# A mixture-of-experts stack: the rows of gate factors of four token chunks, built on TensorE or read back from DRAM

## The chip, the cores and the metric

The kernel runs on one core of a Trainium2 chip. The metric is the time of one execution in device microseconds (us), as the median of several executions. TensorE is called PE in the rows below, its weight loads PEld, VectorE DVE, ScalarE ACT, GpSimd POOL, and SyncE, from whose queue nearly all transfers are issued, SP.

## What is computed

Three stages follow each other: a linear attention with positive random features, a mixture of 8 experts of which each token uses one, and a mixture of 4 experts of which each token uses all. Cut to what matters:

```python
# attention: q, k, v are 2 x 8 x 576 x 64; x becomes 1152 tokens x 512
q_p, k_p = phi(q), phi(k)                       # exp(proj - sq - max) / sqrt(128)
x = (q_p @ (k_p^T @ v)) / (q_p . sum(k_p) + 1e-6)
# first mixture: one expert per token
logits = x @ w_gate;  e_idx = argmax(logits, axis=1)
gate_w = softmax(logits)[e_idx];  eom = sigmoid(x @ w_output_gate)
for e in range(8):
    mask = e_idx == e
    out[mask] = gate_w[mask] * eom[mask, e] * (relu(x[mask] @ w1[e]) @ w2[e])
# second mixture: all four experts
out2 = sum_e p[:, e] * (relu(out @ dw1[e]) @ dw2[e])
```

The change touches the factor `gate_w * eom` of the first mixture alone.

## The kernel before

**Tiling.** The 1152 tokens are two sequences (b = 0, 1) of 576, and each is two chunks of 288, so there are four chunks c = 0..3, with b = c // 2. A chunk is 256 main tokens (two groups of 128) and 32 of the rest. Activations lie turned: features on the 128 partitions, tokens along the row. For the first mixture each sequence has a main expert, the one that most of its tokens chose. The kernel runs the whole chunk through its main expert: `unit1` is the first layer (8 blocks f of 128 hidden features, 12 matmuls of 288 columns each), `unit2` or `unit2_blocks` the second (4 blocks d of 128 output features, 24 matmuls each, tiles `py`). Every product is made as three fp32r matmuls of high and low parts, `mm3`. The result of block d is multiplied by the row of gate factors `gb`, which holds at each token the factor of the main expert, or zero where the token chose another. The same 288 numbers stand on all 128 partitions. Tokens of other experts are added afterwards, by a block for one expert with few tokens (`X`, `second`, `scatter`) and by a loop of a run-time count, which no execution here enters (`tc.If(nx > 0)`, L1186).

**How the row of factors is made.** The gate works with tokens on partitions: `sel_factors` (L586) multiplies the gate values by the main expert's one-hot and sums to `sel`, one column for each group of 128 main tokens and one for the rest. `in_parts` (L580) splits it into a high and a low part. `gate_row` (L910) turns it into a row: ACT scales the rows of an identity by the column, which gives diagonals `dg` (six ACTIVATEs a chunk), PE multiplies them by a matrix of ones (two matmuls, L919, tile `pg`), and ACT copies `pg` to `gb` (L921).

**What sets the order.** A tile framework with a scheduler puts each engine's instructions in a row of its own and adds the semaphore waits; parts of the first stage are chained by hand (`pin`). An engine takes its row in order, and so does SP with its DMAs. Before chunk 0's second layer PE does the last blocks of its first layer, the gate logits of sequence 1, and then mixes matmuls of blocks d = 0 and d = 1 with small matmuls `cps`: one that counts tokens by expert (`cps<-gm_eq`, L503, from DVE's `gm_eq`, L496), and one that needs the one-hot `oh_all`, which DVE's gate chain gives (L573, L575). DVE in that stretch does the low parts `wlo` of the second layer's weights, the gate chain of sequence 1, and chunk 0's products with `gb` (L940). After the branch at L1186, SP loads the second expert's weights (`E1.load2`, L143) for chunk 2.

Of the kernel before, what the change touches and what calls it, by code (L numbers as in the profile page):

```python
# [38 lines left out]
def moe_stack(ctx, tc, q, k, v, omega, w_gate, w_ogate, mw1, mw2, dprobs, dw1, dw2, out):  # L39
# [178 lines left out]
    def load_v(b, hh):  # L218
        raw["v", b, hh] = load_main(v, b, hh, "v", G, D + 1)

    xs = ctx.enter_context(tc.tile_pool(name="dp", bufs=1, space=bass.MemoryType.DRAM)).tile([9, 128, DM], F32, name="xs")
    om2 = cp.tile([128, 2, D], F32, name="om2")
    for r in range(2):
        nc.scalar.dma_start(om2[:, r, :], omega)
# [294 lines left out]
    def gate_math(b, lg, mx, eq, m, cb):  # L519
# [44 lines left out]
        if b == 0:  # L564
            sels = [sel_factors(c, b, eng, pn) for c in range(2)]
            yield
            for c in range(2):
                sel0.append(sels[c]())
        yield

    def gate_count(b, psp, tag):
# [2 lines left out]
                         start=True, stop=True)  # L574
        nc.tensor.matmul(ps[:, :, 2], ones_r, ohr[:, 2 * b:2 * b + 2], start=True, stop=True)  # L575
        nc.vector.tensor_reduce(cnt[:, 2 * b:2 * b + 2], ps.rearrange("p c t e -> p c e t"), axis=AX.X, op=ALU.add)

    sel0 = []

    def in_parts(s, p=lambda i: i):  # L580

        p(nc.vector.tensor_copy(s[:, 0].bitcast(F32R), s[:, 1]))
        p(TT(s[:, 1], s[:, 1], s[:, 0], op=ALU.subtract))
        return s

    def sel_factors(c, b, eng, p=lambda i: i):  # L586
        t = cp.tile([128, 3, NE], F32, tag="selt", name="selt", bufs=2)
        bc = ohb[:, b:b + 1, :]
        p(eng.tensor_tensor(t[:, 0:2], g_all[:, 2 * c:2 * c + 2], bc.to_broadcast([128, 2, NE]), op=ALU.mult))
        p(eng.tensor_tensor(t[:, 2:3], grm[:, c:c + 1], bc, op=ALU.mult))  # L590

        def total():
            s = cp.tile([128, 2, 3], F32, tag="sel", name="sel", bufs=2)
            p(nc.vector.tensor_reduce(s[:, 1], t, axis=AX.X, op=ALU.add))
            return in_parts(s, p)
        return total

    def sel_static(c, b):
        return sel_factors(c, b, nc.vector)() if b else sel0[c]


    units = []
# [326 lines left out]
        return l1(w1, xhc, xlc, *(rings or RINGS))  # L929

    def unit2_blocks(c, w2, hs, late=None):
        gb = gate_row(sel_static(c, c // 2))
        for d in range(KB):
            if d == KB - 1 and late is not None:
                late += [l2_block(w2, hs, d, (ps_k, "kv")), gb]
                yield
                return
            y = l2_block(w2, hs, d, (ps_k, "kv") if (c, d) == (0, 0) else None)
            for dst, src in zip(x2cols(c), (slice(0, 256), slice(256, NC))):
                TT(x2T[:, d, dst], y[:, src], gb[:, src], op=ALU.mult)  # L940
            yield

    def unit2(c, w2, hs):
        if c >= 2:
            gb = gate_row(sel_static(c, c // 2))
            return add_out(w2, hs, gb, list(zip(x2cols(c), (slice(0, 256), slice(256, NC)))))
        for _ in unit2_blocks(c, w2, hs):
            pass

    def x2cols(c):  # L950
        return slice(256 * c, 256 * c + 256), slice(1024 + 32 * c, 1056 + 32 * c)
# [8 lines left out]
    def add_out(w2, hs, gb, cols):  # L960
        for d in range(KB):
            add_yt(l2_block(w2, hs, d), gb, d, cols)
# [84 lines left out]
    for _ in blocks:  # L1047
        pass
    nx_t, mt, le_t, lc_t, sel1, wi_t = extras()
    hs = unit1(1, E0.w1)  # L1050
    pool_x = ExitStack()
    xg_ = pool_x.enter_context(tc.tile_pool(name="xg", bufs=1))
# [133 lines left out]
    with tc.If(nx > 0, preferred_fallthrough_block=True, label="more"):  # L1186
        with tc.For_i(0, nx, 1) as it:
# [18 lines left out]
            add_out(xe.w2, hs, gate_row(in_parts(sx)), [(bass.ds(lc * 256, 256), slice(0, 256)),  # L1206
                                              (bass.ds(lc * 32 + 1024, 32), slice(256, NC))])
    add_yt(*last, KB - 1, list(zip(x2cols(1), (slice(0, 256), slice(256, NC)))))
    pool_l.close()
    pool_o.close()  # L1210
    xq = ctx.enter_context(tc.tile_pool(name="xq", bufs=1, side="right"))
# [2 lines left out]
    E1.load2()  # L1214
    hs = unit1(2, E1.w1)
    unit2(2, E1.w2, hs)
    hs = unit1(3, E1.w1)


# [117 lines left out]
    xc.append(pair_of(xr0, [128, KB, GROUPS[0][1]], ("xch", "xcl")))  # L1337
    x_side(0, nc.vector)()
    w2_ahead = [load_w2(0, 0)]
    gb = gate_row(sel_static(3, 1))  # L1340
    for k in range(2):
        for d in (k, k + 2):
            add_yt(l2_block(E1.w2, hs, d), gb, d, list(zip(x2cols(3), (slice(0, 256), slice(256, NC)))))
# [140 lines left out]
```

## Time and profile before

| | us |
|---|---|
| median of 3 executions | 573.23 (573.07 to 573.31) |
| the profiled execution | 572.74 |
| its span (first to last instruction) | 570.8 |
| around the span | 1.94 |
| PE busy | 562.7 |
| DVE busy | 394.5 |
| ACT busy | 251.1 |
| POOL busy | 263.7 |

The profiled execution is 0.49 us under the median. In the span, attention ends at about 84 us, the first mixture lies from there to about 191 us, and the second mixture takes the rest. PE's busy time counts matmuls that overlap; the start of its weight loads (PEld) tells better at what pace it goes, and a stretch in which they follow each other at an even pace is one in which PE waits for nothing.

### The profile page before, as it was taken

To read this page: it belongs to the slowest core of one execution; us is meant where nothing else is said; L and a number is where in the kernel's file an instruction comes from. 1 tells how busy PE (TensorE), PEld (TensorE's weight loads), DVE (VectorE), ACT (ScalarE), POOL (GpSimd) and SP (SyncE) were. 2 spreads that over 40 slices of the span, in tenths; PEclk is the share of its full clock that TensorE was granted. 3 is DMA by queue.
4 is the path that set the end of the run, shared out by engine and by line. 5 is a ranking of instruction groups with operands and counts; after the bars stand their busy time and mean duration, and the time that the engine had idled before them with its cause. 6 is when DMAs were issued, how large, how long until landed. Compare 5 with 4: busy or idle time off the path is not lost.

```text
span 570.8 us, 11664 instructions
## 1 busy us (share of the span) xinstructions
PE 562.7 (99%) x4526; PEld 510.4 (89%) x4527; DVE 394.5 (69%) x865; ACT 251.1 (44%) x622; POOL 263.7 (46%) x318
## 2 busy tenths in 40 slices
PE   8999999999999999999999999999999999999997
PEld 7787899987999999989989999889988999889996
DVE  7877978946669886666676666666666666665664
ACT  5988844135624534344343443334434344343230
POOL 5996464000100327673663846638456375563210
PEclk9999999999999999999999999999999999999999
DMA  7851560483600400220220021022022002000004
GB/s 179 227 151 40 176 207 1 164 293 116 224 1 5 144 2 2 75 74 1 75 73 1 2 75 73 2 73 75 1 74 75 0 29 85 36 2 1 0 1 165
DMA packets 42473, 42.83 MB, mean 75 GB/s; under 512 B 14896, under 2 KB 31792, under 8 KB 42416
## 3 DMA queue, kind: packets, MB, share of 16 engines
q1 hardware_dynamic: 42128, 42.00, 23.4%
q8 instruction: 36, 0.59, 0.4%
q14 instruction: 21, 0.17, 0.1%
q10 hardware_dynamic: 288, 0.07, 0.1%
HBM read 37.34 MB, written 4.72 MB: 74 GB/s over the span
## 4 chain that ended last, share of the span: by engine, by line
PE 75%; DVE 0%; issue 0%
PE po L646 12%; PE po L645 12%; PE po L647 11%; PE pp L647 10%; PE pp L646 10%; PE pp L645 10%; PE ph L645 2%; PE py L645 2%; PE py L647 1%; PE ph L646 1%; PE ph L647 1%; PE py L646 1%; PE pg L919 0%; DVE ob L1436 0%
## 5 line engine op out<-in xcount | busy, mean ns | idle before, releaser
L105 POOL TENSOR_TENSOR wlo<-st,whi 128x512 fp32r<-128x512 f32 x96 | 115.4, 1222 | 178.1 <-ACT whi L104 134.7
L104 ACT CAST whi<-st 128x512 fp32r<-128x512 f32 x116 | 65.6, 590 | 114.6 <-PE po L647 49.3
L646 PE MATMUL po<-wlo,hh 128*128 128x512 f32 x290 | 112.8, 389 | 0.0
L645 PE MATMUL po<-whi,hh 128*128 128x512 f32 x290 | 112.7, 389 | 0.0
L647 PE MATMUL po<-whi,hl 128*128 128x512 f32 x290 | 112.4, 388 | 0.0
L885 POOL TENSOR_TENSOR hl<-c,hh 128x320 fp32r<-128x320 f32 (+1 forms) x64 | 52.1, 814 | 84.7 <-ACT hh L884 66.7
L647 PE MATMUL pp<-xh,wlo 128*128 128x320 f32 (+1 forms) x256 | 75.8, 296 | 0.0
L646 PE MATMUL pp<-xl,whi 128*128 128x320 f32 (+1 forms) x256 | 75.7, 296 | 0.0
L645 PE MATMUL pp<-xh,whi 128*128 128x320 f32 (+1 forms) x256 | 75.6, 295 | 0.0
L1419 DVE SCALAR_TENSOR_TENSOR oa<-po,pb,oa 128x512 f32<-128x512 f32 x75 | 55.1, 747 | 29.1 <-PE po L647 29.1
L647 PEld LDWEIGHTS po<-whi,hl 128*128 128x128 f32 x290 | 54.5, 188 | 11.4
L645 PEld LDWEIGHTS po<-whi,hh 128*128 128x128 f32 x290 | 54.5, 188 | 10.4
L646 PEld LDWEIGHTS po<-wlo,hh 128*128 128x128 f32 x290 | 54.5, 188 | 10.1
L1419 DVE SCALAR_TENSOR_TENSOR ob<-po,pb,ob 128x512 f32<-128x512 f32 x59 | 44.2, 749 | 26.8 <-PE po L647 26.8
L1374 DVE TENSOR_TENSOR c<-u,pp 128x320 f32<-128x320 f32 (+1 forms) x96 | 43.3, 453 | 22.4 <-PE pp L647 21.9
L883 ACT ACTIVATE c<-c 128x320 f32<-128x320 f32 (+1 forms) x64 | 28.5, 445 | 50.7 <-DVE c L1374 50.0
L646 PEld LDWEIGHTS pp<-xl,whi 128*128 128x128 f32 x256 | 48.5, 190 | 1.2
L645 PEld LDWEIGHTS pp<-xh,whi 128*128 128x128 f32 x256 | 48.5, 190 | 1.2
L647 PEld LDWEIGHTS pp<-xh,wlo 128*128 128x128 f32 x256 | 48.5, 190 | 0.0
L641 DVE SCALAR_TENSOR_TENSOR hl<-c,hh 128x320 fp32r<-128x320 f32 (+1 forms) x64 | 44.4, 724 | 0.5 <-ACT hh L640 0.2
L351 ACT ACTIVATE e<-pj,nb 128x128 f32<-128x128 f32 x144 | 39.1, 392 | 6.6 <-DVE nb L342 6.4
L645 PE MATMUL ph<-xh,whi 128*128 128x288 f32 x128 | 38.2, 299 | 0.4 <-PEq L1186 0.4
(280 smaller groups left out, 1248.9 us busy)
## 6 DMA issues: line engine op xcount, KB each, us to landing
st<-in_moe_w_dram SPq DMA_DIRECT2D x36, 512.0 KB, 4.5
st<-in_moe_w_dram SPq DMA_DIRECT2D x8, 1024.0 KB, 5.7
q<-in_q_dram SPq DMA_DIRECT2D x4, 512.0 KB, 5.3
v<-in_v_dram SPq DMA_DIRECT2D x16, 128.0 KB, 4.9
xs<-xn SPq DMA_DIRECT2D x16, 128.0 KB, 2.5
k<-in_k_dram SPq DMA_DIRECT2D x3, 512.0 KB, 4.5
out_dram<-oa SPq DMA_DIRECT2D x5, 256.0 KB, 2.0
own<-in_moe_w_dram SPq DMA_DIRECT2D x1, 1024.0 KB, 7.3
```

The lines of the kernel that those rows point to most:

```text
L104: p(heng.tensor_copy(hi, src) if heng else nc.scalar.copy(hi, src))
L105: p(eng.tensor_tensor(lo, src, f32(hi), op=ALU.subtract))
L351: pin(nc.scalar.activation(e[:, i], st_p[u][a][:, i], AF.Exp, bias=nb[:, a, i:i + 1]))
L641: return lambda: p(STT(hl, src, 0.0, f32(hh), op0=ALU.max, op1=ALU.subtract))
L645: p(nc.tensor.matmul(ps, sh_, mh, start=start, stop=False))
L646: p(nc.tensor.matmul(ps, sh_, ml, start=False, stop=False))
L647: p(nc.tensor.matmul(ps, sl_, mh, start=False, stop=stop))
L883: nc.scalar.activation(c, c, AF.Relu)
L885: nc.gpsimd.tensor_tensor(hl, c, f32(hh), op=ALU.subtract)
L1374: TT(c, u, p, op=op)
L1419: STT(oacc[T], po, pc, oacc[T], op0=ALU.mult, op1=ALU.add)
```

## The change

`gate_row` stays for the loop alone. For the four chunks, `sel_factors` now ends in a single sum and two small DMAs on SP, which write its three columns to a DRAM tile `gd` of 288 numbers: 256 words from 128 partitions (two from each), and 32 words from 32 partitions. `gate_load` reads that DRAM tile back with one DMA whose source is repeated for all 128 partitions, 128 x 1152 bytes, straight into `gb`. The sums for chunks 2 and 3 are emitted before `unit1(1)`, the load for chunk 2 ahead of `E1.load2()`, and the one for chunk 3 after `unit2(2)`.

```diff
--- before.py
+++ after.py
@@ -218,7 +218,9 @@
     def load_v(b, hh):
         raw["v", b, hh] = load_main(v, b, hh, "v", G, D + 1)
 
-    xs = ctx.enter_context(tc.tile_pool(name="dp", bufs=1, space=bass.MemoryType.DRAM)).tile([9, 128, DM], F32, name="xs")
+    dp = ctx.enter_context(tc.tile_pool(name="dp", bufs=1, space=bass.MemoryType.DRAM))
+    xs = dp.tile([9, 128, DM], F32, name="xs")
+    gd = [dp.tile([1, NC], F32, name=f"gd{c}") for c in range(4)]
     om2 = cp.tile([128, 2, D], F32, name="om2")
     for r in range(2):
         nc.scalar.dma_start(om2[:, r, :], omega)
@@ -565,7 +567,7 @@
             sels = [sel_factors(c, b, eng, pn) for c in range(2)]
             yield
             for c in range(2):
-                sel0.append(sels[c]())
+                sels[c]()
         yield
 
     def gate_count(b, psp, tag):
@@ -575,8 +577,6 @@
         nc.tensor.matmul(ps[:, :, 2], ones_r, ohr[:, 2 * b:2 * b + 2], start=True, stop=True)
         nc.vector.tensor_reduce(cnt[:, 2 * b:2 * b + 2], ps.rearrange("p c t e -> p c e t"), axis=AX.X, op=ALU.add)
 
-    sel0 = []
-
     def in_parts(s, p=lambda i: i):
 
         p(nc.vector.tensor_copy(s[:, 0].bitcast(F32R), s[:, 1]))
@@ -590,13 +590,17 @@
         p(eng.tensor_tensor(t[:, 2:3], grm[:, c:c + 1], bc, op=ALU.mult))
 
         def total():
-            s = cp.tile([128, 2, 3], F32, tag="sel", name="sel", bufs=2)
-            p(nc.vector.tensor_reduce(s[:, 1], t, axis=AX.X, op=ALU.add))
-            return in_parts(s, p)
+            s = cp.tile([128, 3], F32, tag="sel", name="sel", bufs=2)
+            p(nc.vector.tensor_reduce(s, t, axis=AX.X, op=ALU.add))
+            r = slice(32 * c, 32 * c + 32)
+            nc.sync.dma_start(gd[c][0, 0:256].rearrange("(t p) -> p t", p=128), s[:, 0:2])
+            nc.sync.dma_start(gd[c][0, 256:NC].rearrange("(p o) -> p o", o=1), s[r, 2:3])
         return total
 
-    def sel_static(c, b):
-        return sel_factors(c, b, nc.vector)() if b else sel0[c]
+    def gate_load(c):
+        g = gp.tile([128, NC], F32, tag="gb", name="gb")
+        nc.sync.dma_start(g, gd[c].partition_broadcast(128))
+        return g
 
 
     units = []
@@ -929,7 +933,7 @@
         return l1(w1, xhc, xlc, *(rings or RINGS))
 
     def unit2_blocks(c, w2, hs, late=None):
-        gb = gate_row(sel_static(c, c // 2))
+        gb = gate_load(c)
         for d in range(KB):
             if d == KB - 1 and late is not None:
                 late += [l2_block(w2, hs, d, (ps_k, "kv")), gb]
@@ -942,8 +946,7 @@
 
     def unit2(c, w2, hs):
         if c >= 2:
-            gb = gate_row(sel_static(c, c // 2))
-            return add_out(w2, hs, gb, list(zip(x2cols(c), (slice(0, 256), slice(256, NC)))))
+            return add_out(w2, hs, gbs.pop(0), list(zip(x2cols(c), (slice(0, 256), slice(256, NC)))))
         for _ in unit2_blocks(c, w2, hs):
             pass
 
@@ -1047,6 +1050,8 @@
     for _ in blocks:
         pass
     nx_t, mt, le_t, lc_t, sel1, wi_t = extras()
+    for c in (2, 3):
+        sel_factors(c, 1, nc.vector)()
     hs = unit1(1, E0.w1)
     pool_x = ExitStack()
     xg_ = pool_x.enter_context(tc.tile_pool(name="xg", bufs=1))
@@ -1206,6 +1211,7 @@
             add_out(xe.w2, hs, gate_row(in_parts(sx)), [(bass.ds(lc * 256, 256), slice(0, 256)),
                                               (bass.ds(lc * 32 + 1024, 32), slice(256, NC))])
     add_yt(*last, KB - 1, list(zip(x2cols(1), (slice(0, 256), slice(256, NC)))))
+    gbs = [gate_load(2)]
     pool_l.close()
     pool_o.close()
     xq = ctx.enter_context(tc.tile_pool(name="xq", bufs=1, side="right"))
@@ -1214,6 +1220,7 @@
     E1.load2()
     hs = unit1(2, E1.w1)
     unit2(2, E1.w2, hs)
+    gbs.append(gate_load(3))
     hs = unit1(3, E1.w1)
 
 
@@ -1337,7 +1344,7 @@
     xc.append(pair_of(xr0, [128, KB, GROUPS[0][1]], ("xch", "xcl")))
     x_side(0, nc.vector)()
     w2_ahead = [load_w2(0, 0)]
-    gb = gate_row(sel_static(3, 1))
+    gb = gbs.pop(0)
     for k in range(2):
         for d in (k, k + 2):
             add_yt(l2_block(E1.w2, hs, d), gb, d, list(zip(x2cols(3), (slice(0, 256), slice(256, NC)))))
```

On PE, at the start of chunk 0's second layer, before (`py_2007` is block d = 0, `py_2063` block d = 1; the numbers behind the names are buffers):

```order
L645 MATMUL py_2007<-hh_1759,whi_1864 128x288
L646 MATMUL py_2007<-hl_1760,whi_1864 128x288
L647 MATMUL py_2007<-hh_1759,wlo_1865 128x288
L919 MATMUL pg_2002<-dg_1995,ones_80 128x288 x2
L645 MATMUL py_2007<-hh_1811,whi_1935 128x288
L646 MATMUL py_2007<-hl_1812,whi_1935 128x288
L645 MATMUL py_2063<-hh_1614,whi_1806 128x288
```

and the same place now (`py_2001` is d = 0, `py_2057` is d = 1; the change moves the lines of the file by a few):

```order
L649 MATMUL py_2001<-hh_1763,whi_1868 128x288
L650 MATMUL py_2001<-hl_1764,whi_1868 128x288
L651 MATMUL py_2001<-hh_1763,wlo_1869 128x288
L649 MATMUL py_2001<-hh_1815,whi_1939 128x288
L650 MATMUL py_2001<-hl_1816,whi_1939 128x288
L649 MATMUL py_2057<-hh_1618,whi_1810 128x288
```

The two matmuls `pg` are gone and nothing stands in their place; the other three chunks lose their two in the same way.

On PE, further on in chunk 0's second layer, where the matmuls `cps` on DVE's one-hot stand, before (`py_2090` is block d = 2):

```order
L645 MATMUL py_2063<-hh_1898,whi_1947 128x288
L646 MATMUL py_2063<-hl_1899,whi_1947 128x288
L647 MATMUL py_2063<-hh_1898,wlo_1948 128x288
L645 MATMUL py_2090<-hh_1614,whi_1806 128x288
L646 MATMUL py_2090<-hl_1615,whi_1806 128x288
L573 MATMUL cps_2059<-oh_all_96,ones_80 128x2x16
L575 MATMUL cps_2059<-ohr_98,ones_80 128x2x8
```

and now (`py_2084` is block d = 2):

```order
L649 MATMUL py_2057<-hh_1902,whi_1951 128x288
L650 MATMUL py_2057<-hl_1903,whi_1951 128x288
L651 MATMUL py_2057<-hh_1902,wlo_1952 128x288
L649 MATMUL py_2084<-hh_1618,whi_1810 128x288
L650 MATMUL py_2084<-hl_1619,whi_1810 128x288
L651 MATMUL py_2084<-hh_1618,wlo_1811 128x288
L649 MATMUL py_2084<-hh_1618,whi_1829 128x288
L575 MATMUL cps_2053<-oh_all_96,ones_80 128x2x16
L577 MATMUL cps_2053<-ohr_98,ones_80 128x2x8
```

Both `cps` stand two products of the second layer later than before; there are 17 products between the first `cps` (on `gm_eq`) and this one in both.

In SP's row, behind the last load of sequence 0's weights, before (`TENSOR_LOAD` reads the number of sequence 1's main expert, then the counts for the loop and the expert with few tokens):

```order
L143 DMA st_1797<-in_moe_w2_dram 128x4x512
L1212 TENSOR_LOAD ei1_1971
L1212 ISA x2
L1185 TENSOR_LOAD nx_2183
L1185 ISA x2
L1053 TENSOR_LOAD wi_2181
```

and now:

```order
L143 DMA st_1801<-in_moe_w2_dram 128x4x512
L596 DMA gd0_136<-sel_1872 128x2x1
L597 DMA gd0_136<-sel_1872 32x1
L596 DMA gd1_137<-sel_1876 128x2x1
L597 DMA gd1_137<-sel_1876 32x1
L602 DMA gb_1999<-gd0_136 128x288
L602 DMA gb_2517<-gd1_137 128x288
L1218 TENSOR_LOAD ei1_1975
L1218 ISA x2
L596 DMA gd2_138<-sel_2204 128x2x1
L597 DMA gd2_138<-sel_2204 32x1
L596 DMA gd3_139<-sel_2211 128x2x1
```

Writes and reads of chunks 0 and 1 stand ahead of the first register load, and the writes of chunks 2 and 3 between the first and the second.

## Rows read from the trace of the kernel before

**Rows 1.** Page: busy time by engine, and the granted clock in 40 slices.
```profile
PE 562.7 (99%) x4526; PEld 510.4 (89%) x4527; DVE 394.5 (69%) x865; ACT 251.1 (44%) x622; POOL 263.7 (46%) x318
...
PEclk9999999999999999999999999999999999999999
```

**Rows 2.** Chain that ended last by engine; all of PE's waits between 84 and 200 us.
```profile
PE 75%; DVE 0%; issue 0%
...
PE ph L645 <- PEq L1186: 0.4, 1, 0.4
```

**Rows 3.** Instructions of L919 and L915: ns min/median/max, first and last start in us.
```profile
L919 PE MATMUL pg<-dg,ones x8: 292/294/381, 91.8 to 178.2; 128*128 128x288 f32 x8
...
L915 ACT ACTIVATE dg<-ident,sel x16: 386/389/415, 87.7 to 154.9; 128x128 fp32r<-128x128 f32 x16
```

**Rows 4.** Timeline of PEld around `pg`, chunks 0 and 2: start us, us, instruction.
```profile
91.49 0.19 PEld L647 LDWEIGHTS py<-hh,wlo 128*128 128x128 f32 x1
91.77 0.30 PEld L919 LDWEIGHTS pg<-dg,ones 128*128 128x128 f32 x2
92.01 0.19 PEld L645 LDWEIGHTS py<-hh,whi 128*128 128x128 f32 x1
...
152.05 0.32 PEld L919 LDWEIGHTS pg<-dg,ones 128*128 128x128 f32 x2
152.32 0.19 PEld L645 LDWEIGHTS py<-hh,whi 128*128 128x128 f32 x1
```

**Rows 5.** Timeline of DVE, then PEld, in chunk 0's second layer; idle before in brackets.
```profile
91.19 0.46 DVE L641 SCALAR_TENSOR_TENSOR hl<-ph,hh 128x288 fp32r<-128x288 f32 x1 [0.37 <-ACT hh L640]
...
93.70 0.68 DVE L105 TENSOR_TENSOR wlo<-st,whi 128x512 fp32r<-128x512 f32 x1
...
94.52 0.20 DVE L496 TENSOR_TENSOR gm_eq<-lg,gm_mx 128x40 fp32r<-128x40 f32 x1
...
95.03 0.42 DVE L940 TENSOR_TENSOR x2T<-py,gb 128x256 f32<-128x256 f32 x1 [0.20 <-PE py L647]
...
97.03 0.17 DVE L553 CAST oh_all<-gm_oh 128x32 fp32r<-128x32 f32 x1
...
94.52 0.32 PEld L647 LDWEIGHTS py<-hh,wlo 128*128 128x128 f32 x2
94.78 0.19 PEld L503 LDWEIGHTS cps<-gm_eq,ones 128*128 128x128 f32 x1
...
97.02 0.19 PEld L646 LDWEIGHTS py<-hl,whi 128*128 128x128 f32 x1
97.32 0.19 PEld L573 LDWEIGHTS cps<-oh_all,ones 128*128 128x128 f32 x1
```

**Rows 6.** Timeline of DVE: chunk 0's factors are summed.
```profile
87.31 0.18 DVE L594 TENSOR_REDUCE sel<-selt 128x3 f32<-128x24 f32 x1
```

**Rows 7.** DMA issues: KB each, median us to landing; `xs` from 78 to 84 us.
```profile
xs<-xn SPq DMA_DIRECT2D x2, 128.0 KB, 1.9
...
v<-in_v_dram SPq DMA_DIRECT2D x16, 128.0 KB, 4.9
...
wg<-in_moe_w_gate_dram SPq DMA_DIRECT2D x1, 16.0 KB, 2.0
```

**Rows 8.** Timeline of SP's DMA issues, and SP's wait at L143 (total, times, longest).
```profile
80.91 0.40 SPq L143 DMA_DIRECT2D st<-in_moe_w_dram  x1
...
138.09 1.52 SPq L143 DMA_DIRECT2D st<-in_moe_w_dram  x2
...
SPq L143 <- DVEq L1186: 9.9, 1, 9.9
```

**Rows 9.** Timeline of ACT, DVE and PEld in chunk 2's first layer.
```profile
143.97 2.18 ACT L104 CAST whi<-st 128x512 fp32r<-128x512 f32 x4 [0.66 <-DMA st<-in_moe_w_dram]
...
147.04 0.81 DVE L641 SCALAR_TENSOR_TENSOR hl<-ph,hh 128x288 fp32r<-128x288 f32 x2
...
149.02 0.19 PEld L646 LDWEIGHTS ph<-xl,whi 128*128 128x128 f32 x1
```

## The prediction

> **What bounds the kernel now.** I read the busy times first. PE is busy for 99% of the span at a granted clock of full speed throughout (2.4 GHz, the upper of its two levels), DVE for 69%, ACT for 44% [rows 1]. The chain that ended last runs over PE alone, and the waits view of the stretch that the change touches, 84 to 200 us, lists one wait of PE, 0.4 us at the branch [rows 2]. So a microsecond taken from PE's row is a microsecond of the kernel, unless something else is then late; one taken from ACT or DVE is worth nothing by itself. Busy times are too long for pricing a matmul, since matmuls overlap: the eight `pg` show 294 ns each [rows 3], 2.35 us in all. I price by the starts of PE's weight loads instead, and then ask at each place where PE listens to DVE, ACT or a DMA whether it now arrives too early.
>
> **The matmuls that go.** In chunk 2 the pair starts at 152.05 and the next product at 152.32, so it costs 0.27 us [rows 4]. Chunks 1 and 3 lose the same pair at a place where PE is fed evenly: 3 x 0.27 = 0.81 us. In chunk 0 the last product before the pair loads at 91.49; at the pace of half a pair, 0.13, the next would load at 91.62, but it loads at 92.01 [rows 4]. The pair costs 0.39 there: 0.26 of its own and 0.13 of waiting for DVE's `hl`, which ends at 91.19 + 0.46 = 91.65 [rows 5] and frees the bank that `pg` is given. Upper bound of all four: 0.39 + 0.81 = 1.20.
>
> **What is late next in chunk 0.** DVE's chain does not move with PE, so a part comes back.
> First `cps`, on `gm_eq`. Two more products stand before it now: PE would be there at 94.78 - 0.39 + 0.26 = 94.65. But `gm_eq` ends at 94.52 + 0.20 = 94.72, and the `cps` of before began 0.06 behind it, at 94.78 [rows 5]. It begins at 94.78 again, two products further on: 0.26 is kept and 0.13 lost.
> Second `cps`, on `oh_all`, 17 products later in both orders. Before, PE was ready at 97.02 + 0.13 = 97.15 and began at 97.32: it waited 0.17 for `oh_all`, which ends at 97.03 + 0.17 = 97.20 [rows 5]. Now it is ready at 97.15 again, and what counts is when DVE gets there. DVE's chain was held at L940 for 0.20 by block d = 0, whose last product loads at 94.52, 0.51 ahead of L940 at 95.03 [rows 5]. That product needs the last `wlo`, which ends at 93.70 + 0.68 = 94.38; 0.06 behind that is 94.44, so L940 goes at 94.95 and everything behind it 0.08 earlier. The second `cps` begins at 97.24, and chunk 0 gains 0.26 + 0.08 = 0.34.
> Sum on PE: 0.34 + 0.81 = **1.15 us less**.
>
> **ACT and DVE lose work too.** Sixteen ACTIVATEs of 389 ns [rows 3], the eight smaller ones and the four copies go from ACT, eight small operations of `in_parts` from DVE. I put this at nothing: PE waits for neither in the waits view [rows 2], and in chunk 0 the DVE chain is tied to the weights and to block d = 0, not to the removed operations. At most it would return the 0.13 and the 0.09 that I let PE wait at the two `cps`, 0.22 more.
>
> **The row through DRAM.** It adds, for each chunk, two writes of single words and a read, on SP. In chunk 0 the read has to land before L940 at 94.95. The trace has no DMA of 4-byte pieces and none that repeats its source, so I bound each step by rows. `sel` is summed at 87.31 + 0.18 = 87.49 [rows 6]; SP's last issue before it was at 80.91 [rows 8], so its queue is empty. The two writes go at 87.55 and, by the 0.40 of an issue [rows 8], at 87.95. The read cannot be issued before both have landed. For the writes the nearest row is the gate weights, 16 KB in pieces of 32 bytes, 2.0 us to landing; for the read of 147 KB it is `xs`, 128 KB on an idle system, 1.9 us. The high end for either is `v`, 128 KB behind a full queue, 4.9 us [rows 7]; below 1.9 I see no row for anything. I take 2.0 and 2.2, since the queue is empty: landed at 87.95 + 2.0 + 2.2 = 92.15, which is 2.8 us early. At the high end it is 87.95 + 4.9 + 4.9 = 97.75, which is 2.8 us late. What hides the round trip is the rest of chunk 0's first layer and block d = 0; L940 is its first reader.
> The Trainium skill, page "DMA: Bandwidth & Descriptors", section "Rules for kernel authors", speaks against the writes: a strided or non-contiguous last dimension goes out as one descriptor per element, and transfers under 64 KB pay mostly overhead. The section "Specifications" adds that pieces under 512 B are written by read-modify-write. No row shows what a 4-byte write costs, so here the pages only name the mechanism of the second rival below; the sum stays with the rows.
>
> **What is queued behind the new DMAs.** SP waits for `gd` to land before each read, and behind that stands the register load of sequence 1's expert, which waits for DVE until after L940 anyway. The four writes of chunks 2 and 3 stand ahead of the next register loads, which wait for values that DVE makes later. After the branch the read for chunk 2 stands ahead of the second expert's weights. SP issued those at 138.09, on being released by DVE's arrival at the branch (9.9 us of waiting) [rows 8]; DVE gets there with PE's scatter, so some 0.6 us earlier now (chunk 0's and chunk 1's gain), and one issue of 0.40 in front costs nothing. Were it 1 us late, ACT's first part at 143.97 would be (it waited 0.66 for the DMA), then DVE's `hl` behind it at 147.04; PE wants the bank of that `hl`, free at some 147.5, only at 149.02 [rows 9], 1.5 us later. Nothing. The read for chunk 3 waits for chunk 1's last product with `gb`, the first thing that DVE does after the branch, and nothing due soon stands behind it.
>
> **The rivals.**
> One: chunk 0 gives nothing back to PE, or DVE, which is close behind PE at both `cps`, holds it further on as well. For it: two places within 2.6 us where PE is already at DVE's pace [rows 5]. Against it: the chunks 1 to 3 have no such place in the waits view [rows 2]. It leaves 0.81 or less: 572.74 - 0.81 = 571.9 for the profiled execution, 572.4 as a median; if all is given back, 573.2.
> Two, on the other side: chunk 0's row lands late. L940 stands in DVE's row ahead of the whole gate chain, so the second `cps` moves with it, at 97.24 + (landing - 94.95), and PE stops there one for one. The gain is gone when the row lands 1.15 late, at 96.1, that is when write and read take 4.1 us each; at the high end, 2.8 late, the kernel is 1.65 slower, 574.9. For it: single words, and 128 reads of the same 1152 bytes, neither of which the trace shows. Against it: 2.8 us of slack, and an idle system.
> The page's rule on one descriptor per element would act here and nowhere else, since only chunk 0's row is made close to its use.
> Three: the gain is larger, because DVE and ACT are lighter and both waits at `cps` vanish: 1.15 + 0.22 = 1.37 saved, 571.9.
> That the change does not do what it says I leave aside: the order shows no `pg` for any of the four chunks.
>
> **How the numbers follow.** The profiled execution would take 572.74 - 1.15 = 571.6. It stands 0.49 below the median of 573.23, and I take the change off the median: 573.23 - 1.15 = **572.1 us**. A measurement of this kernel can tell about 0.2% from no change, 1.15 us, so the forecast lies on that line itself and its sign of significance is open. Chances: forecast, with 1.0 to 1.25 saved, 0.70, of which 0.38 falls beyond 0.2% and 0.32 within; rival one 0.14, all within; rival two 0.09, of which 0.06 is slower by over 0.2% and 0.03 within; rival three 0.05, faster; a loss in SP's queue 0.02, half of it slower. That gives 0.43 faster, 0.50 the same, 0.07 slower. The range takes in the forecast, rival three and rival one down to a saving of 0.3: 571.7 to 572.9. Its upper end leaves out rival two.
>
> **What would show it.** Right: no `pg` in the trace; the first `cps` of chunk 0's second layer still 0.06 behind `gm_eq`; second `cps` near 97.2; L940 released by PE's `py`, not by a DMA; everything from 200 us on earlier by 1.1 to 1.2. Wrong: L940 waiting for the DMA of `gb`, and PE then idle at `cps<-oh_all`, for rival two; a landing of `gd` far above 2 us would explain it. An end that moves by 0.8 with chunk 0 unmoved is rival one. If PE waits for weights at the start of chunk 2's second layer, my reading of SP's queue was wrong.

## The result, and the profile after

The changed kernel takes 580.48 us (median of 4 runs, 580.14 to 581.19) against 573.26 (573.07 to 573.31) for the kernel before: 1.0127 times as long, 95% interval 1.0115 to 1.0140, or 7.2 us. The forecast was 572.1 us. The profiled execution of the changed kernel took 580.26 us, its span is 578.5; line numbers in its rows are those of the changed kernel, where L940, L573 and L1106 of before are L944, L575 and L1111. Its page, in the parts that answer to [rows 1] and to the chain in [rows 2]:

```profile
PE 564.3 (98%) x4518; PEld 510.9 (88%) x4519; DVE 394.0 (68%) x857; ACT 243.5 (42%) x594; POOL 264.0 (46%) x318
...
PEclk9999999799999999999999999999999999999999
...
PE 90%; DMA 3%; DVE 3%; ACT 1%; POOL 1%; issue 1%; SPq 1%; POOLq 0%; ACTq 0%; DVEq 0%
```

PE has 8 matmuls fewer, as forecast, and 1.6 us more of busy time. Two things are new: DMA stands in the chain that ended last, with 3% of the span, and one of the 40 slices has a granted clock of 0.7. Both lead to 100 us. The waits view of 84 to 210 us has two lines there that the kernel before does not have (waiter, what it waited for, us in total, times, longest):

```profile
DVE x2T L944 <- DMA gb<-gd: 6.5, 1, 6.5
PEld cps L575 <- DVE oh_all L555: 6.4, 1, 6.4
```

This is rival two of the prediction: L944, DVE's first product with `gb`, waits for the DMA of `gb`, and PE waits at the second `cps` behind it. SP's DMA issues, DVE and PE's weight loads at that place (start, us, engine, line; idle before in brackets):

```profile
87.83 0.38 SPq L596 DMA_DIRECT2D gd<-sel  x1
88.26 0.46 SPq L597 DMA_DIRECT2D gd<-sel  x1
...
96.49 0.94 SPq L602 DMA_DIRECT2D gb<-gd  x2
...
94.95 0.19 DVE L527 TENSOR_TENSOR gm_d<-lg,gm_mx 128x40 f32<-128x40 f32 x1
101.64 0.42 DVE L944 TENSOR_TENSOR x2T<-py,gb 128x256 f32<-128x256 f32 x1 [6.50 <-DMA gb<-gd]
...
103.64 0.17 DVE L555 CAST oh_all<-gm_oh 128x32 fp32r<-128x32 f32 x1
...
97.30 0.19 PEld L649 LDWEIGHTS py<-hh,whi 128*128 128x128 f32 x1
103.86 0.29 PEld L575 LDWEIGHTS cps<-oh_all,ones 128*128 128x128 f32 x1 [6.38 <-DVE oh_all L555]
...
107.10 0.29 PEld L650 LDWEIGHTS py<-hl,whi 128*128 128x128 f32 x1
107.33 0.19 PEld L651 LDWEIGHTS py<-hh,wlo 128*128 128x128 f32 x1
107.47 0.19 PEld L649 LDWEIGHTS py<-hh,whi 128*128 128x128 f32 x1
```

The words went out at 87.83 and 88.26, within 0.3 us of the forecast. The read could be issued only at 96.49, that is 8.2 us behind the second write, and its row reached DVE at 101.6. In the same stretch the DMA engines do next to nothing. The DMA view from 87.5 to 97 us in 40 slices of 0.24 us (busy share in tenths), and its issues (KB each, median us to landing):

```profile
DMA  0000050005000000000000000000000000000000
...
gb<-gd SPq DMA_DIRECT2D x1, 144.0 KB, 5.0
gd<-sel SPq DMA_DIRECT2D x2, 1.0 KB, 8.2
```

All 640 packets are moved in two short bursts before 90 us. So it is not the sending that takes 6 us more, but what follows until the writes count as landed.

Where the 7.7 us of span come from, by the starts of PE's weight loads in the two traces. The extra expert is the one with few tokens; `px` are the products on its x, and `xt` is that x, which SP loads back from DRAM.

| place | after | before | us |
|---|---|---|---|
| second `cps`, on `oh_all` | 103.86 | 97.32 [rows 5] | +6.54, of which 0.31 was there before the change acts (an earlier product at 86.65 and 86.34) |
| the 16 loads from 103.86 on, to 107.47 | 3.61 | 16 x 0.132 = 2.11 | +1.5, granted clock at half |
| two products that stood behind the second `cps` and now stand ahead of it | done | 2 x 0.132 to come | -0.26 |
| the same product once the clock is back | 107.33 | 99.51 | +7.82 measured; the three above make 7.8 |
| first product behind the extra expert's `px` | 128.37 | 119.63 | +8.74 measured: 0.92 more, in two waits between the loads of `px` (0.47 and 0.53) |
| chunk 1's pair | gone | 0.27 | -0.27 |
| first product behind the branch | 147.96 | 139.43 | +8.53 measured; the sum makes 8.5 |
| pairs of chunks 2 and 3 | gone | 0.54 | -0.54: 8.0, which the products of the second mixture keep to their end |

What follows PE's last load is 0.3 us shorter than before, so the span is 7.7 longer and not 8.0.

Two windows show the second row (us of the window, busy time of PE, PEld, DVE, ACT, POOL with counts, granted clock, DMA share, GB/s):

```profile
100.50:107.30 6.80, 3.43 (x14) 3.44 (x15) 5.31 (x47) 0.00 (x0) 0.00 (x0) 0.50 0.11 16
107.40:110.00 2.60, 2.60 (x22) 2.60 (x21) 1.29 (x8) 0.00 (x0) 0.00 (x0) 1.00 0.07 1
```

PE stood idle for 6.4 us, and the granted clock fell at 100.5, while it was idle; from its return at 103.86 the loads follow one another by 0.24 us, at a granted clock of 0.50, which is 1.2 GHz, and from 107.33 by 0.13 again, at 2.4.

### The profile page after: what moved, and what is told of

Its sections match the earlier page's. It is cut to its first block, busy times and chain, and to the rows that moved or that the text cites. A ratio compares the mean times of both kernels' runs of the same rounds, so it can differ in the third digit from the quotient of the medians.

```text
span 578.5 us, 11624 instructions
## 1 busy us (share of the span) xinstructions
PE 564.3 (98%) x4518; PEld 510.9 (88%) x4519; DVE 394.0 (68%) x857; ACT 243.5 (42%) x594; POOL 264.0 (46%) x318
## 4 chain that ended last, share of the span: by engine, by line
PE 90%; DMA 3%; DVE 3%; ACT 1%; POOL 1%; issue 1%; SPq 1%; POOLq 0%; ACTq 0%; DVEq 0%
PE po L649 11%; PE po L650 11%; PE po L651 11%; PE pp L649 10%; PE pp L651 10%; PE pp L650 10%; PE py L649 3%; PE py L650 3%; PE ph L649 3%; PE py L651 3%; PE ph L650 3%; PE ph L651 3%; PE pj L325 2%; PE pnd L414 2%; PE kv L365 2%; DMA gd<-sel 1%
## 5 line engine op out<-in xcount | busy, mean ns | idle before, releaser
L104 ACT CAST whi<-st 128x512 fp32r<-128x512 f32 x116 | 65.6, 590 | 117.2 <-PE po L651 49.3
L649 PE MATMUL py<-hh,whi 128*128 128x288 f32 x128 | 38.9, 305 | 0.0
```

The lines of the kernel that those rows point to most:

```text
L104: p(heng.tensor_copy(hi, src) if heng else nc.scalar.copy(hi, src))
L649: p(nc.tensor.matmul(ps, sh_, mh, start=start, stop=False))
```

## The experiments

Three questions were open. Is chunk 0's row the whole loss? Why do two writes of 1.1 KB need 8 us? And is the saving of 1.15 us there at all? Twelve kernels were run; each median stands against the kernel before on the same chip, 573.1 to 573.4 us.

### One chunk or all

The first run gives chunk 0 its old row and leaves the rest of the change.

```
-        gb = gate_load(c)
+        gb = gate_load(c) if c else gate_row(sel0[0])
         (sel0: one more tile of 24 bytes, split in parts as before)
```

> Chunk 0's row is made as before (diagonals and two products of ones), chunks 1 to 3 go through DRAM as in the changed kernel. Theory 1, the whole loss is chunk 0's row, which lands 6.5 us after DVE wants it: no wait of DVE for gb, PE waits for nothing at the second cps beyond the 0.17 of before, TensorE granted full speed in 100 to 110 us, and three pairs of 0.27 us saved: 573.26 - 0.81 = 572.4 us. Theory 2, the DMAs of the other chunks (words on SP's queue ahead of weights and register loads) cost something of their own as well: 574 us or more, with a new wait of PE behind 120 us.

577.69 us, 1.0071 (1.0057 to 1.0084). The stall at `cps` is gone, but 4.3 us stay. Two things in the trace were new. PE waits 2.6 us at `px`, 2.4 more than before. And the 128x512 products of the second mixture take longer, with no wait and at full clock. This run had a fault of its own: its extra tile moves all that lies behind it in SBUF by 32 bytes. So it was repeated with the numbers in the two tiles that are there anyway:

```
-                s = cp.tile([128, 2, 3], F32, name="sel0")
+            s = cp.tile([128, 2, 3], F32, tag="sel", name="sel", bufs=2)
```

> Again chunk 0's row as before and chunks 1 to 3 through DRAM; the one difference from the run on chunk 0 is that the three numbers of each partition lie in the two tiles of 24 bytes that the kernel before has, so that no later tile moves in SBUF. In that run the 128x512 products of the second mixture followed one another by 0.233 us, before by 0.226, and PE waited 2.2 us more at px, where the extra expert's x landed 8.6 us after its issue, 5.2 before. Theory 2a, the slower products come from the moved addresses and the wait from the word writes of chunks 2 and 3, issued 7 us ahead of the extra expert's loads: pitch back at 0.226, xt still landing after 8 us or more, PE still waiting some 2 us at px, 574.5 to 575.2 us. Theory 2b, the writes cost both: 577.7 us as there. Theory 1, neither is from the writes: 572.5 us.

574.5 us, 1.0021 (1.0011 to 1.0030): theory 2a, the products are back at their old pace, and PE still waits. SP's issues and PE's loads in that kernel, and the times from issue to landing of the extra expert's x (`xt`):

```profile
99.68 0.36 SPq L602 DMA_DIRECT2D gd<-sel  x1
...
102.00 0.46 SPq L603 DMA_DIRECT2D gd<-sel  x1
106.90 1.11 SPq L138 DMA_DIRECT2D st<-in_moe_w_dram  x2
112.70 1.04 SPq L1070 DMA_DIRECT2D xt<-xs  x2
113.79 0.43 SPq L1071 DMA_DIRECT2D xt<-xs  x1
...
120.23 0.14 PEld L1117 LDWEIGHTS px<-xt,og 128*32 128x32 f32 x2 [1.60 <-DVE ds__2417 L966]
120.91 0.14 PEld L1117 LDWEIGHTS px<-xt,og 128*32 128x32 f32 x2 [0.54 <-DVE pb L967]
121.58 0.14 PEld L1117 LDWEIGHTS px<-xt,og 128*32 128x32 f32 x2 [0.54 <-issue]
```

```profile
DMA to landing us min/median/max: 7.4/7.5/7.7
```

PE's waits at `px` add up to 2.7 us, 2.5 more than before. The last part of x, issued at 113.79, lands at 113.79 + 7.5 = 121.3, just ahead of the third `px`: the view names a DVE operation, but that had long been done, and it was the DMA. In the kernel before, x lands 5.2 us after its issue, ahead of `px`. The loads are 7 us behind the word writes of chunks 2 and 3. GB/s from 104 to 130 us in 40 slices of 0.65 us, first this kernel, whose weights were issued at 106.90, and then the next one below, at 106.91:

```profile
GB/s 0 13 0 0 0 0 44 32 38 38 167 85 72 145 359 397 403 410 406 406 378 375 391 388 397 384 391 384 384 391 378 344 66 25 9 66 227 403 403 406
```

```profile
GB/s 13 0 0 0 0 0 98 236 403 413 406 407 394 397 394 378 391 375 337 388 375 369 391 403 255 60 236 325 249 9 0 95 205 394 413 403 394 413 403 378
```

With the words ahead of them, the loads crawl at 32 to 167 GB/s until 113 us; without them they are at 403 from 109.2 on. The second kernel has only chunk 1's row in DRAM, and so no words at that time:

```
+        gb = gate_load(c) if c in (1,) else gate_row(rows[c])
         (chunks 2 and 3: sel_factors and gate_row at the place of before)
```

> Only chunk 1's row goes through DRAM, chunks 0, 2 and 3 have theirs made as before, at the place of before. Its words are written near 89 us, 17 us ahead of the next loads, and nobody wants its row before 125 us. Theory 2a: the loads issued at 106.4 move at once, xt lands 5.2 us after its issue, no new wait of PE, one pair saved: 573.36 - 0.27 = 573.1 us. Rival, a round trip through DRAM costs something even when nothing is near it: 574 us or more.

572.93 us, 0.9997 (0.9988 to 1.0007), expected 573.1; x lands after 5.0 us (median) and PE has no new wait at `px`. A round trip that nobody waits for, with nothing behind it, costs nothing. The price of chunk 0 alone comes from the reverse:

```
+        gb = gate_load(c) if c in (0,) else gate_row(rows[c])
```

> Only chunk 0's row goes through DRAM, as words, chunks 1 to 3 have theirs made as before. It gives the price of chunk 0 alone. Theory: writes of 8.2 and a read of 4.9 us as in the changed kernel, so DVE waits 6.5 us for gb, PE 6.4 us at the second cps, the granted clock falls to half for some 3.3 us (1.35 us lost), one pair saved (0.34): 573.1 + 6.25 + 1.35 - 0.34 = 580.3 us. Rival, half of the landing was due to chunk 1's words, which were in flight with chunk 0's: the row lands 3 to 4 us sooner, 576 to 577 us.

579.54 us, 1.0105 (1.0088 to 1.0122). The rival falls: the words take 8.1 us also without chunk 1's. The terms were each somewhat off: the read took 4.2 us in place of 4.9, so PE waited 5.3 us and not 6.4; but the granted clock was low from 101.2 to 108.0, in the changed kernel from 100.5 to 107.3. PE came back at 102.86, and not at 103.86, so more of its work fell into the low stretch: the 22 loads from 102.86 to 108.02 took 5.16 us in place of 22 x 0.132 = 2.9. That is 2.3 us lost to the clock, against 1.5 in the changed kernel. The window of the low stretch, as above:

```profile
101.20:108.00 6.80, 5.13 (x21) 5.14 (x22) 4.84 (x48) 0.00 (x0) 0.00 (x0) 0.50 0.00 0
```

### Why the words take 8 us

Behind the last result, single DMAs were chained on idle queues, each waiting for the one ahead.

```
+    nc.sync.dma_start(p1[0, :].rearrange("(t p) -> p t", p=128), db[:, 0:2])
+    nc.sync.dma_start(da, p1.partition_broadcast(128))
     ... and so on; what one writes the next one reads
```

> The changed kernel with a chain of single DMAs behind its last result, each waiting for the one ahead, on idle queues: a write of 128 pieces of 1 KB and its read; 256 words side by side as in the change, and a read of that 1 KB by all partitions; 32 words; 128 words; 128 pieces of 8 bytes; 256 words 64 bytes apart, read back as words; 256 words 512 bytes apart, read back as words; one piece of 1 KB; 128 pieces of 32 bytes; one single word; and 256 words side by side once more. Its time means nothing, the landings do. Theory A, the number of pieces sets a write's landing: 256 words 8 us wherever they lie, 128 pieces of 4, 8 or 32 bytes some 5, 32 words 3, one word 2. Theory B, neighbouring words in one line of DRAM wait for one another: 256 words side by side 8 us, 64 or 512 bytes apart 2 to 3, 128 pieces of 32 bytes 2 to 3. Theory C, it was what else moved at that time: all writes land in 2 to 3 us here.

> A second chain of single DMAs behind the last result, each waiting for the one ahead; again only the landings mean anything. 256 words side by side and two reads of that 1 KB by all partitions, one after the other; one piece of 1 KB and its read by all partitions; 256 words at steps of 8, 16, 32 and 64 bytes; 128 pieces of 12, 16 and 24 bytes side by side; 256 words side by side with a read of 128 x 992 bytes of another place issued right behind them, and the same with words 64 bytes apart. Theory B, neighbours in one line of 64 bytes wait for one another: some 8 us at a step of 4, half of it at 8, a quarter at 16, 2 us at 64; 12, 16 and 24 bytes 2 to 3. Theory 2a, the unfinished words hold up what is queued behind them: the read behind the words side by side lands after 6 us or more, the one behind the spread words after 2 to 2.5; rival, a read passes them: 2 us both times. The first read of a row made of words takes longer than the second (5.4 against 2 to 3) if the writes were still being finished; the same for both if it is the 128 readers of one place.

SP's timeline of the first chain; an issue waits for the landing ahead, so the difference of two starts is the earlier one's price:

```profile
578.98 0.32 SPq L1477 DMA_DIRECT2D db<-p  x1
580.99 0.37 SPq L1478 DMA_DIRECT2D p<-db  x1
589.20 0.32 SPq L1479 DMA_DIRECT2D da<-p  x1
594.64 0.32 SPq L1480 DMA_DIRECT2D p<-da  x1
...
617.89 0.61 SPq L1486 DMA_DIRECT2D p<-db  x1
619.98 0.58 SPq L1487 DMA_DIRECT2D da<-p  x1
```

At 578.98 stands the read of 128 rows of 1 KB (2.0 us), at 580.99 the 256 words side by side (8.2), at 589.20 the read of that 1 KB by all partitions (5.4), at 617.89 the 256 words 64 bytes apart (2.1). From the second chain:

```profile
588.60 0.32 SPq L1476 DMA_DIRECT2D da<-q  x1
593.27 0.32 SPq L1477 DMA_DIRECT2D da<-q  x1
596.13 0.28 SPq L1478 DMA_DIRECT2D q<-da  x1
597.23 0.35 SPq L1479 DMA_DIRECT2D db<-q  x1
600.37 0.37 SPq L1480 DMA_DIRECT2D q<-db  x1
603.25 0.37 SPq L1481 DMA_DIRECT2D da<-q  x1
```

The first two are the reads of such a KB of words by all partitions, one after the other (4.7 and 2.9), at 596.13 stands 1 KB in one piece (1.1), at 597.23 its read (3.1), at 600.37 the words at a step of 8 bytes (2.9). Of its DMA issues (KB, us to landing), the read that was issued right behind 256 words:

```profile
da<-q SPq DMA_DIRECT2D x1, 124.0 KB, 7.5
```

All prices of the two chains, by such differences, each from one execution:

| write to DRAM | us |
|---|---|
| 256 words side by side (three times) | 8.2, 8.4, 8.1 |
| 128 words; 32 words; one word | 7.6; 3.1; 1.0 |
| 256 words at steps of 8, 16, 32 bytes | 2.9, 1.55, 1.6 |
| 256 words at steps of 64, 512 bytes | 2.1 and 1.6, 2.0 |
| 128 pieces of 8, 12, 16 bytes, side by side | 3.7, 2.3, 1.4 |
| 128 pieces of 24, 32 bytes, side by side | 1.4, 1.4 |
| one piece of 1 KB; 128 pieces of 1 KB | 1.1; 1.85 |

Theory A falls: 256 words take 1.55 us when they are 16 bytes apart, so the number of pieces is not the price. Theory C falls: it is as slow on idle queues. Theory B holds, with a smaller unit than I had guessed: a step of 16 bytes is already free, one of 8 costs 1.3 us, and neighbouring words 6.6. What lands slowly are pieces under 16 bytes that lie side by side. Why that is so stays open, and so does why 128 such words take nearly as long as 256 and 32 less than half.

Two more prices hang on it. The read of the 1 KB by all partitions takes 4.7 us the first time and 2.9 the second; behind a row that was written in one piece it takes 3.1. So some 2 us of the read, too, belong to the words before it. And a read of 128 x 992 bytes of another place, issued 0.44 us behind 256 words, lands after 7.5 us, where the like read alone takes 2.0: theory 2a's hold-up, in the open. GB/s of that read, issued at 627.27 behind words side by side, from 626.5 to 635.5 us in 40 slices of 0.225 us, and then of the one behind words 64 bytes apart, issued at 638.37, from 638 to 642.5 us in 40 slices of 0.11 us:

```profile
GB/s 0 0 0 0 0 3 2 0 119 159 110 0 0 0 0 0 0 0 0 18 0 48 22 4 13 35 9 4 4 9 9 0 0 0 0 0 0 0 0 0
```

```profile
GB/s 0 0 0 0 0 0 0 2 7 1 0 0 0 26 71 106 159 265 344 150 9 0 1 4 4 0 0 0 0 0 0 0 0 0 0 0 0 0 0 0
```

Behind words side by side some 90 of the 124 KB move by 629.0 and the rest only between 630.8 and 633.5, so a load crawls rather than stands. Behind words 64 bytes apart all of it has moved by 640.4, 2.0 us after the issue; its landing is not on record. All these DMAs were issued from SP's queue; whether one from another queue is held up as well was not tried.

The Trainium skill, page "DMA: Bandwidth & Descriptors", section "Specifications", says that transfers under 512 B per piece make the engine read, modify and write. Here that is not the price by itself: one word lands in 1.0 us and words 16 bytes apart in 1.55. The section "Rules for kernel authors" of that page of the Trainium skill has a non-contiguous last dimension go out as one descriptor per element; the 640 packets for the 576 words of four DMAs are about one a word and agree, but they were moved by 90 us and their number is not what was waited for.

### The change with longer pieces

So the same change was built with the three numbers of a partition side by side: one write of 128 pieces of 12 bytes for each chunk, a row of 384 numbers that the products read with a step of three.

```
-            nc.sync.dma_start(gd[c][0, 0:256].rearrange("(t p) -> p t", p=128), s[:, 0:2])
-            nc.sync.dma_start(gd[c][0, 256:NC].rearrange("(p o) -> p o", o=1), s[r, 2:3])
+            nc.sync.dma_start(gd[c][0].rearrange("(p t) -> p t", t=3), s)
```

> The changed kernel with another layout of the row in DRAM: the three numbers of a partition stand side by side, so that a chunk's write is one DMA of 128 pieces of 12 bytes, in place of two with 288 pieces of 4; the row that is read back has 384 numbers (96 of them unused), and the products read it with a step of three, yt in two pieces. From the chain of single DMAs (128 pieces of 8 bytes landed after 3.7 us, of 32 bytes after 1.4, 256 words after 8.2) the write lands after some 2.7 us and the row near 96 us. Theory B, neighbouring pieces in one line wait for one another: DVE waits for gb near 1 us in place of 6.5, the clock stays at full speed, the loads behind chunk 2's and 3's writes move at once, 573 us, give or take 0.6. Theory A, it is the DMA itself or its wait, whatever the pieces: 578 us or more.

571.98 us, 0.9976 (0.9967 to 0.9986): faster than before, by 1.1 to 1.4 us, and by 0.4 more than the expectation allowed. SP, DVE and PE at the place of the stall, and the DMA issues from 87 to 97 us:

```profile
88.11 0.80 SPq L595 DMA_DIRECT2D gd<-sel  x2
90.67 0.80 SPq L600 DMA_DIRECT2D gb<-gd  x2
...
95.46 0.49 DVE L947 TENSOR_TENSOR x2T<-py,gb 128x256 f32<-128x256 f32 x1
...
97.76 0.19 PEld L575 LDWEIGHTS cps<-oh_all,ones 128*128 128x128 f32 x1
```

```profile
gb<-gd SPq DMA_DIRECT2D x2, 192.0 KB, 3.8
gd<-sel SPq DMA_DIRECT2D x2, 1.5 KB, 2.3
```

The write lands after 2.3 us and the read after 3.8, so chunk 0's row is there at 94.4. L947 begins at 95.46, 0.04 behind the DVE operation ahead of it, and waits for no DMA; a wait of 1 us had been expected. Everything in this execution is 0.60 late from before the change acts, so the second `cps` stands at 97.16 on the scale of [rows 5]. The loads behind chunk 2's and 3's writes land x after 5.1 us.

### The order in DVE's row

The other way out is to let the row be late. Here the first two products with `gb` are written behind the gate work of sequence 1, with the words as in the change:

```
             y = l2_block(w2, hs, d, (ps_k, "kv") if (c, d) == (0, 0) else None)
+            if c == 0 and d == 0:
+                yield
```

> The changed kernel with one thing moved: the first two products with gb are written behind the gate work of sequence 1, so that in DVE's row they stand behind oh_all and no longer ahead of it. The row lands as late as in the changed kernel, at 101.6 us. Theory 1, the stall reaches PE only through the second cps: DVE still waits for gb, some 4 us, PE does not wait at cps, since four banks (kv and three of pj) take blocks d = 0 to 3, 94.9 + 3 x 24 x 0.132 = 104.4 us, before PE needs one back; granted clock full; 572.1 us, up to 573.3 if DVE's backlog is felt at px. Theory 2, PE stops in any case, for a bank or for work that DVE does too late: 576 us or more.

580.04 us, 1.0117 (1.0102 to 1.0132): no better than the change. Yet the first half of theory 1 came true. DVE waits 4.7 us for `gb`, but `oh_all` is through before that, and the second `cps` loads at 96.59 without a wait. The stall has moved on to the extra expert, as its waits and its window of 120 to 130 us show:

```profile
PE px L1113 <- DMA xt<-xs: 5.1, 1, 5.1
...
DVE x2T L946 <- DMA gb<-gd: 4.7, 1, 4.7
```

```profile
120.00:130.00 10.00, 5.39 (x26) 2.60 (x30) 1.53 (x7) 0.98 (x2) 0.00 (x0) 0.66 0.96 351
```

What DVE does behind the wait names that expert, so its x is issued at 115.26 in place of 111.08, and behind the words of chunks 2 and 3 it takes 9.3 us to land; then the clock falls again. Some 1.5 us more go in two smaller waits ahead of that, at 110.8 and 117.6, for work that DVE does late. To part the two, chunks 2 and 3 got their old rows:

```
+        gb = gate_load(c) if c in (0, 1) else gate_row(rows[c])
         (and the yield ahead of the first products, as above)
```

> The version with the gate work ahead of the first product with gb, but with the rows of chunks 2 and 3 made as before: no words are written ahead of the extra expert's loads. In the version with all four chunks PE waited 5.1 us for that expert's x, which was issued 4.2 us later than before (DVE stood 4.7 us at gb ahead of the work that names the expert) and took 9.3 us to land in place of 5.2. Here it is issued as late but lands after 5.2: PE waits some 1 us at px, and with one pair less the two-chunk saving of 0.6 is eaten up: 573 to 574 us, clock full. If PE still waits 4 us or more there, the words of chunks 2 and 3 were not the cause of the late landing.

575.09 us, 1.0031 (1.0021 to 1.0042). x lands 5.3 us after its issue, so the words were the cause of the 9.3. But PE waits 2.6 us at `px` and not some 1, and the time is beyond the 573 to 574 us expected: x was issued 3.8 us late, and the slack that I had counted on is only 1 us (before, x lands at 112.04 + 5.2 = 117.2, and `px` begins at 118.30). With both repairs, the edits of the long pieces and of the order in one kernel:

> The 12-byte layout, and the first two products with gb behind the gate work of sequence 1 in DVE's row. Theory 2a and B together: neither the row of chunk 0 nor the loads come late, PE waits nowhere that it did not before, and the saving of the run without any row is there: 572.4 us. If something else of the change still costs, 573.4 or more.

571.82 us, 0.9975 (0.9965 to 0.9985), no different from the long pieces alone. Once the row lands in time, the order is worth nothing.

### What the saving is

```
-        nc.sync.dma_start(g, gd[c].partition_broadcast(128))
-        return g
+        return f32(xh[:, 0, 0:NC])        (and no writes to gd)
```

> Leaves out the gate factors of the four chunks: no row is made or moved at all, and the products with gb read the first 288 columns of the high part of x in its place, which has long been there. It measures what the eight products of ones and their company cost PE, the term of 1.15 us in the forecast. Theory 1: 573.26 - 1.15 = 572.1 us, the second cps near 97.2 us, nothing waiting for gb. Rival, DVE gives the saving back further on (chunk 0 gains nothing or little): 572.4 to 573.2 us.

572.49 us, 0.9986 (0.9977 to 0.9995). Every product with `gb` reads the first columns of x, so this is the price of the row in the kernel before, with no DMA put in its place. The second `cps` loads at 97.23, in an execution that was 0.11 late before it. Behind the branch 0.71 us are won on the same scale; later PE waits 0.66 for DVE's `c` at 195.96, which takes back about what chunks 2 and 3 give. The long pieces have no such wait and win 1.1 to 1.4.

### The 32 bytes

The first run's other loss was tried by itself, on the kernel before:

```
     cp.tile([128, 64], F32, name="even")
+    cp.tile([128, 8], F32, name="shift")
```

> The kernel before with one unused tile of 32 bytes per partition added, so that the operands and weights of all later stages lie 32 bytes further on in SBUF, at odd multiples of 32 in place of multiples of 64; no instruction is added or moved. The two versions with chunk 0's row as before differed in this alone, and by 3.2 us: 577.69 against 574.5. If the addresses did it: 573.3 + 3.2 = 576.5 us, the 128x512 products of the second mixture at 0.233 us in place of 0.226 in part of it, PE never waiting more than before. If not: 573.3 us.

576.51 us, 1.0050 (1.0033 to 1.0067): 3.2 us for an unused tile. One of the three lines of 128x512 products, by form, here and then in the kernel before (count, busy us, mean ns):

```profile
L647 PE MATMUL po<-wlo,hh 128*128 128x512 f32 x286 | 112.3, 393 | 0.0
```

```profile
L646 PE MATMUL po<-wlo,hh 128*128 128x512 f32 x286 | 111.6, 390 | 0.0
```

The three lines together take 2.3 us more. Not all products are slower: 466 of 839 neighbouring ones start 0.230 us or more after the one ahead, against 124 before. The first run, with its extra tile, shows the same (468). But the expectation that PE never waits more than before failed. In the profiled execution PE waits 1.4 us more at 16.2 us, in the attention, and 0.6 in two waits for DVE's `hl` in chunk 2. The first run has neither, so whether the tile caused these is open. The traces show no addresses, so where the operands lie is not shown.

## Why the prediction was wrong, step by step

- **What bounds the kernel; ACT and DVE work at nothing.** Right in the main. Without any row the second `cps` has no wait left, 0.12 earlier than forecast, where at most 0.09 was allowed for it; no run tells whether that is the lighter DVE.
- **The matmuls that go, 1.15 us.** Right in kind and near in size. The long pieces save 1.1 us by the medians and 1.4 by the ratio; without any row the first `cps` stands at 94.88 - 0.11 = 94.77 (forecast 94.78) and the second at 97.12 (forecast 97.24), so chunk 0 gives 0.46 rather than 0.34. Rival one is true only of the run without a row, in small.
- **The row through DRAM, landed at 92.15.** This is the step that failed. The writes were priced at 2.0 us by the gate weights, 16 KB in pieces of 32 bytes [rows 7]. They took 8.2. Both rows of the estimate go the other way: `wg` is a load from DRAM and was taken for the write, `xs` is a write to DRAM and was taken for the read. The row that I chose has pieces of 32 bytes, and a write of such pieces takes 1.4; neighbouring words are another thing, and no row of before has them. The prediction said so, and then let the 4.9 of another row stand as the upper bound. There was no reason for that: 4.9 belongs to big loads behind a full queue and says nothing of words. An operation that the trace does not show had no upper bound, and the range and the 0.09 for rival two were made as if it had. The read was priced at 2.2 and took 5.0, near the bound of 4.9; some 2 us of it come from the words.
- **Rival two.** Its place, its mechanism and its point of decision were right: the second `cps` moves with the landing, 97.24 + (101.6 - 94.95) = 103.9, measured 103.86. Its price was not: 1.65 at the high end, because the landing was bounded at 97.75, and because the forecast had no term for the clock, which takes 1.5 us more once PE has stood idle for 6.4.
- **What is queued behind the new DMAs, at nothing.** Wrong, and not seen in any rival. I asked what SP waits for and issues later, and not what is in flight on the DMA engines. The writes of chunks 2 and 3 cost SP 2 us of issue that nobody misses, but with chunk 0 as before, x behind them is issued 1.1 us later (112.70, less the 0.49 that this execution was late before, against 111.08) and lands 2.3 us later (7.5 against 5.2): PE waits 2.5 us more at `px` than before. In the changed kernel x is held up too, by 1.8 us (7.0 against 5.2), and PE's 0.9 at `px` stand at that place.
- **The second expert's weights** behind the read for chunk 2 cost nothing, as forecast: PE has no wait at chunk 2's second layer.

## What to carry to other kernels

When a change brings in a kind of transfer that the trace does not hold, a long landing of another kind is not its upper bound: time it by itself first, or give the case in which it is late the chance that ignorance deserves. A row of numbers goes to DRAM in pieces of 12 bytes or more, or at steps of 16, not as neighbouring words; and the loads that come behind such writes have to be counted, as well as the read that waits for them. When a wait is put into an in-order engine's row, look at everything behind it: moving its first reader back only carried the loss to the next thing that the same engine feeds.

## What was unexpected of the hardware

- Neighbouring pieces under 16 bytes: 256 words side by side land after 8.1 to 8.4 us, at a step of 16 bytes after 1.55. Their packets are gone by then; the DMA engines show as idle for 6 us.
- While such a write is unfinished, DMAs issued behind it from the same queue are held up: a read of 124 KB lands after 7.5 us, and 2 MB of weights move at 32 to 167 GB/s in place of 400 until 13 us after the first word was issued. The first read of the written row takes 4.7 us, the second 2.9.
- An unused tile of 32 bytes, which moves the later operands in SBUF, cost 0.5% of the kernel. In the trace 2.3 us of it are 128x512 products that take 393 ns on the mean in place of 390. An experiment that adds a small tile can measure this in place of what it is meant to.
- After an idle time of 6.4 us PE ran at the lower clock for 3.5 us, and after one of 5.3 us for 5.2: the shorter pause cost more clock. In both the clock fell while PE was idle, at 100.5 and 101.2 us, and rose at 107.3 and 108.0; PE came back at 103.86 and 102.86, so after the shorter pause more work lay in the low stretch.
